# Two 512-column weight pieces in place of four, and the second block's transposes ahead of the first gate quarters

## The chip, the cores and the metric

The kernel runs on one core of one Trainium2 chip. The metric is the device time of one execution in microseconds. The kernel before took 236.01 us, the median of three runs that went from 235.99 to 237.07.

## What is computed

Three parts are added: the input x itself, a long convolution gated by the normalized input (part A), and a gated pair of projections (part B). S is 2048 rows, D is 640, F is 1728, all in bf16.

```python
def _A_ref(q, k, v, shift_k, ssm_k, ssm_D):
    ...
    for t in range(ks):
        k_shift = k_shift + k_pad[:, t:t + S, :] * shift_k[:, ks - 1 - t][None, None, :]
    kv = k_shift * v
    ...                    # y: kv convolved with ssm_k along S, by FFT over 2S
    y = y + kv * ssm_D[None, None, :]
    return q * y

def _B_ref(x, w_gate, w_up, w_down):
    g = jnp.einsum("bsd,df->bsf", x, w_gate)
    u = jnp.einsum("bsd,df->bsf", x, w_up)
    h = _sigmoid(g) * u
    return jnp.einsum("bsf,fd->bsd", h, w_down)

x = A_q
xn = _layernorm(x, axis=-1)
return x + _A_ref(xn, A_k, A_v, A_shift_k, A_ssm_k, A_ssm_D) + _B_ref(xn, B_w_gate, B_w_up, B_w_down)
```

## The kernel before

**Part B.** The 2048 rows are 16 blocks of 128. Four blocks make a group (t = 0 to 3). For a group, xn is transposed into xnT (for each block five pieces of 128 channels), and for each of 13 slices of 128 weight columns (fc) there is a gate product and an up product, each five matmuls of 128x512 (product, L260), into tiles pg and pu of the PSUM ring psG, which has four buffers. ScalarE takes the sigmoid of pg (gate_ev, L269), VectorE multiplies it by pu into hT (up_ev, L275). A last slice holds the remaining 64 columns of both matrices (both_mm, L281). Then hT goes through w_down (down_mm, L304), and VectorE adds the result to x (L309). Weights stay in SBUF: w holds gate and up columns, wd the rows of w_down.

**Part A.** The columns are five chunks of 128 (c). VectorE makes kv from k, the taps sc and v (kv_op, L337 to L346) and turns the filter hn (h_turn, L323). The convolution is done by transforms on TensorE in two steps each way (st1_mm L363 and L365, st2_mm L396, inv1_mm L425, inv2_mm L464), evicted by ScalarE (L223) or VectorE (L226), with trips through DRAM between them on SP's queue (wr1 L377, rd2 L387, wr2 L441, rdb L455).

**The start.** SP and ScalarE load the four blocks of group 0 (L479, L481). SP then loads the weight columns 0 to 255 and 256 to 511 of gate and of up (load_w, L173 and L176). TensorE has nothing to do yet: busy(10), L491, issues ten matmuls on a zeroed tile whose result is not used. VectorE normalizes the four blocks one after the other: statistics (L198), their mean (L202), the variance (L210), the power -1/2 on GpSimd (L214), and xn (ln_xn, L219). turn(i) is five transposes of block i on TensorE (xn_mm, L233) and a copy of their PSUM tile into xnT by ScalarE (xn_ev, L236). For group 0 the first two weight slices are not done as five matmuls of 512 columns but in quarters of 128 columns, one block at a time (quarter, L251), so that they can begin before all four blocks are there: quarters(0, i) is ten gate matmuls of block i, quarters(1, i) ten up matmuls. On TensorE the order is: turn(0), five more matmuls of busy, quarters(0,0), turn(1), quarters(0,1), turn(2), quarters(1,0), quarters(1,1), turn(3), quarters(0,2), quarters(1,2), quarters(0,3), quarters(1,3). Then the products of slice 2 begin. ScalarE's copy for block 1 is what quarters(0,1) waits for.

**The order of the rest.** Every later step belongs to a chain that is named by a letter: g are TensorE's products, s and u their evictions, m the first loads on SP's queue, l the normalization and so on. A string, ORDER, written out by hand, says whose next step is issued; each engine executes its steps in that order. The chain m holds the loads of the weight columns from 512 on (in pieces of 256, gate and up in turn), the taps sraw of chunk 0 (load_taps, L143), the small table SMt, w_down, k (L155, L159, L160), the filter, v, the table S1t and the next group's x (L129). SP's queue also carries the transposes of xn for the later groups (xn_turn, L240).

Of the kernel before, what the change touches and what calls it, by code (L numbers as in the profile page):

```python
# [57 lines left out]
def kernel(  # L58
# [62 lines left out]
    sync = nc.sync  # L121
# [108 lines left out]
    def xn_mm(i):  # L230
        xts[i] = pt = psC.tile([P, NC, P], BF16, name="pt", tag="c")
        for c in range(NC):
            nc.tensor.transpose(pt[:, c, :], xn[:, i, c * P:(c + 1) * P], ident[:])  # L233

    def xn_ev(i):
        nc.scalar.copy(out=xnT[:, i, :, :], in_=xts[i][:, :, :])  # L236
# [8 lines left out]
    def quarter(u, fc, i):  # L245

        if i == 0:
            pgs[u, fc] = psG.tile([P, 512], F32, name=("pg", "pu")[u], tag="g")
        o = u * UP + fc * P
        for c in range(NC):  # L250
            nc.tensor.matmul(pgs[u, fc][:, i * P:(i + 1) * P], lhsT=w[:, c, o:o + P], rhs=xnT[:, i, c, :],  # L251
                             start=(c == 0), stop=(c == NC - 1))
# [236 lines left out]
    def busy(n):  # L489
        for _ in range(n):  # L490
            nc.tensor.matmul(idle[:, :], lhsT=hT[:, 0, 0:P], rhs=hT[:, 0, :], start=True, stop=True)  # L491

    def turn(i):
        xn_mm(i)
        xn_ev(i)
# [9 lines left out]
        ln_pow(0, i, i + 1)  # L505
    ln_xn(0, 3)
    turn(0)
    busy(5)
    def quarters(u, i):
        quarter(u, 0, i)  # L510
        quarter(u, 1, i)

    for i in range(2):
        quarters(0, i)
        turn(i + 1)
    for i in range(2):
        quarters(1, i)
    turn(3)
    for i in range(2, 4):
        for u in range(2):  # L520
            quarters(u, i)
# [7 lines left out]
    def step(k, fn, *args):  # L529
        chains[k].append((fn, args))  # L530
# [16 lines left out]
    def hs(c):  # L547
        return [(load_h, c)]

    def ks(c):  # L550
        return [(load_halo, c), (load_k, c, 0, 8), (load_k, c, 8, NB)]

    def vs(c):
        return [(load_v, c, 0, 8), (load_v, c, 8, NB)]

    for k in ((load_w, sync, 512, 768, 0),
              (load_w, sync, 512, 768, 1),
              (load_taps, 0),
              (sync.dma_start, SMt[:], SMd.ap()),
              (load_w, sync, 768, 1024, 0),  # L560
              (load_w, sync, 768, 1024, 1),
              (load_w, sync, 1024, 1280, 0),
              (load_w, sync, 1024, 1280, 1),
              (load_wd, sync, 0, 7),
              *ks(0),
              (load_w, sync, 1280, FF, 0),
              (load_w, sync, 1280, FF, 1),
              *hs(0),
              *vs(0),
              (load_wd, sync, 7, NFC),  # L570
              (sync.dma_start, S1t[:], S1d.ap()),
              *hs(1),
              (load_x, sync, 1),
              *ks(1),
              *vs(1)):
        step("m", *k)
# [59 lines left out]
    step("o", store, NB - 1, NB, 4 * P, DM)  # L636

    ORDER = """
    mmggmmsmgmmuggmsgmgsuZumgggssumkgkguskugkkmsgugmmmmgkgmksgmuggHskkHkgsmukkgDumsgggkusumgmkgkukagaumH
    gTlllAKlglAatkwuAmmmakPlAkgalAklkwgalggagkegeugADkkaeAaAgewaugkuAHkuggkAukTkwsgKkgkkgnustakguKKgghal  # L640
    AsukwAsakggrluglsaksAugHggkAVubkkkBlswKBukgggaTVsgpkuslukawgDkHPlngAaAaskgAKrwAkukgspbgtkkBsllBugauA
    kgagpsAaguswVpakAguhkHHAgrgDkwcgVklguCkkraeCagAgkAbuBkuBkkggKgkbBKpggBaeualwukkggeIuurlTlAegkwtVbBBg
    gagkAagppswuAaghkuaKswgpAAkaHAskWgHupDgakuVsAggswucglJukkgkrClrsbngpBugaBaAgAWkkgsbspugPkrBgwpgsRFku
    kgprcwgCJusgbgusgpuBdBWppbqrgsdBlrRuqgBcqlCggJbsggksuBupgllkBbBgrqkWBgeaaeAAuppwdgaduRegaIAgrugpaAqa
    eqggupAwcCqpJguugdbgFBgbBqqgugBppdcpWCuJqgrpsgqbgBsuwFgrgqsbuBgpBRsuWgpdcpqqdguJgqCsrrbFBgsgRbugBBpd
    rsppugcdCqugCqgbsgWBqpqggusrBRbpudgrgqWspBpBqcupdJsgCbgRBpgBqqguWgsppuqscCudgJsguqgqgRdWgoquuqoddRgg
    gRqquqguoqoggdoouqdgdqgqdqqqugoggqqugoooouooo
    """
    left = {k: iter(v) for k, v in chains.items()}
    for k in "".join(ORDER.split()):  # L650
# [33 lines left out]
```

## Time and profile before

| what | value |
|---|---|
| median of three runs | 236.01 us |
| the profiled execution, its own time | 236.98 us |
| its span, from the first to the last instruction | 235.2 us |
| TensorE busy | 229.1 us (97%) |
| TensorE weight loads | 131.3 us (56%), beside the matmuls |
| VectorE busy | 204.5 us (87%) |
| ScalarE busy | 121.4 us (52%) |
| GpSimd busy | 12.4 us (5%) |
| moved by DMA | 56.79 MB, mean 241 GB/s |
| first product of 512 columns starts | 13.93 us |

Busy time is that of an engine's instructions; a TensorE matmul's end is modelled, since matmuls overlap in the pipe, so the spacing of their starts tells the pace better than their durations. PEclk in the page is the granted clock in tenths. The profile is of one execution; its time differs from the median of the runs by 0.97 us, so sums are made in the profiled execution and carried over as differences. In rows of the timeline the first number is the start in us from the start of the span, the second the duration, xN the number of instructions merged into the row, and the brackets hold the engine's idle time before the row and what ended it.

### The profile page before, as it was taken

Reading aid. Unit: us, or ns where it says so; the run is one execution under the profiler, and the core shown is the slowest. Engines: PE = TensorE matmul, PEld = TensorE weight load, DVE = VectorE, ACT = ScalarE, POOL = GpSimd, SP = SyncE. Lnnn points to the kernel's source line nnn. Section 1 sums busy time; section 2 is a strip of 40 time slices with the busy share of each in tenths; the row PEclk is TensorE's granted clock in tenths of the full one; section 3 lists DMA queues with packets and bytes.
Section 4 is the critical chain, followed back from the end, with each engine's and each line's share of the span. In section 5 each row is a group of like instructions: output and inputs, shape, how many; then the busy total and the mean of one; then the engine's idle time right before and its main releaser. Section 6 shows DMA issues by size and latency. Waiting matters only on the chain. (4 is left out here: it accounts for less than half of the span.)

```text
span 235.2 us, 5440 instructions
## 1 busy us (share of the span) xinstructions
PE 229.1 (97%) x2203; PEld 131.3 (56%) x2203; DVE 204.5 (87%) x364; ACT 121.4 (52%) x152; POOL 12.4 (5%) x24
## 2 busy tenths in 40 slices
PE   7899999999999999999999999999999999999995
PEld 2764445777454545677564544468754444446772
DVE  4633799999979999999999999997889999897773
ACT  2342332463555788575586747674446667762000
POOL 5210010020001010000000300000000000000000
PEclk9999999999999999999999999999999999999999
DMA  6999999698899999989899989986999777876884
GB/s 184 292 310 247 273 299 290 182 263 146 217 284 291 229 337 236 291 201 258 221 200 300 281 238 300 257 230 183 280 212 316 190 216 204 210 188 171 236 258 134
DMA packets 97615, 56.79 MB, mean 241 GB/s; under 512 B 55926, under 2 KB 91830, under 8 KB 97334
## 3 DMA queue, kind: packets, MB, share of 16 engines
q1 hardware_dynamic: 97158, 56.12, 90.9%
q10 hardware_dynamic: 432, 0.33, 0.7%
q8 instruction: 17, 0.28, 0.5%
q14 instruction: 8, 0.07, 0.1%
HBM read 36.12 MB, written 18.35 MB: 232 GB/s over the span
## 5 line engine op out<-in xcount | busy, mean ns | idle before, releaser
L260 PEld LDWEIGHTS <-w 128*128 128x128 bf16 x500 | 46.7, 98 | 54.4 <-issue 4.8
L304 PE MATMUL pd<-wd,hT 128*128 128x320 bf16 (+2 forms) x448 | 66.0, 299 | 0.0
L260 PE MATMUL pg<-xnT,w 128*128 128x512 bf16 x250 | 62.2, 379 | 0.2 <-ACT sig L269 0.2
L260 PE MATMUL pu<-xnT,w 128*128 128x512 bf16 x250 | 62.2, 379 | 0.0
L304 PEld LDWEIGHTS <-hT 128*128 128x128 bf16 x448 | 41.7, 98 | 18.2 <-issue 2.4
L223 ACT CAST t<-ps 128x1024 bf16<-128x1024 f32 x38 | 37.5, 1014 | 26.1 <-PE ps L365 15.2
L269 ACT ACTIVATE sig<-pg 128x512 bf16<-128x512 f32 x52 | 31.1, 602 | 28.7 <-PE pg L260 23.4
L275 DVE TENSOR_TENSOR hT<-sig,pu 128x512 bf16<-128x512 bf16 x52 | 35.0, 680 | 11.6 <-PE pu L260 7.5
L223 ACT CAST xz<-ps 128x1024 bf16<-128x1024 f32 x36 | 35.1, 1015 | 15.7 <-PE ps L396 15.6
L411 DVE TENSOR_TENSOR xz<-xz 128x2048 bf16<-128x2048 bf16 x20 | 24.4, 1220 | 0.2
L363 PE MATMUL ps<-kvh,S1t 128*128 128x128 bf16 x160 | 21.5, 218 | 0.6 <-ACT t L223 0.4
L365 PE MATMUL ps<-kvh,S1t 128*128 128x128 bf16 x160 | 21.6, 220 | 0.0
L343 DVE TENSOR_TENSOR acc<-acc,tmp 128x1024 bf16<-128x1024 bf16 x30 | 20.5, 684 | 0.3
L341 DVE TENSOR_TENSOR tmp<-kx,sc 128x1024 bf16<-128x1024 bf16 x30 | 20.4, 681 | 0.3
L309 DVE TENSOR_TENSOR x<-pd,x 128x320 bf16<-128x320 f32 (+2 forms) x32 | 15.2, 482 | 3.8 <-PE pd L304 3.6
L363 PEld LDWEIGHTS <-S1t 128*128 128x128 bf16 x160 | 15.5, 97 | 3.9 <-DVE kvh L346 1.6
L365 PEld LDWEIGHTS <-S1t 128*128 128x128 bf16 x160 | 15.4, 96 | 2.4
L198 DVE BATCH_NORM_STATS2 st<-x 128x6 f32<-128x320 bf16 x32 | 13.9, 475 | 2.5 <-DMA x<-in_A_q_dram 2.5
L469 DVE TENSOR_TENSOR yx<-psb,xn 128x512 bf16<-128x512 f32 x20 | 13.7, 686 | 1.4 <-PE psb L464 0.8
L409 DVE STREAM_SHUFFLE xz<-xz 128x512 f32<-128x512 f32 x20 | 14.5, 727 | 0.0
L223 ACT CAST ao<-psa 128x1024 bf16<-128x1024 f32 x9 | 9.0, 1013 | 8.4 <-PE psa L425 6.9
L464 PEld LDWEIGHTS <-TBt 128*128 128x128 bf16 x160 | 9.9, 98 | 3.4 <-issue 1.8
(48 smaller groups left out, 150.1 us busy)
## 6 DMA issues: line engine op xcount, KB each, us to landing
d<-t SPq DMA_DIRECT2D x20, 512.0 KB, 4.3
t<-d SPq DMA_DIRECT2D x20, 512.0 KB, 6.9
bi<-d SPq DMA_DIRECT2D x8, 512.0 KB, 4.7
d<-ao SPq DMA_DIRECT2D x6, 512.0 KB, 5.8
kx<-in_A_k_dram SPq DMA_DIRECT2D x10, 256.0 KB, 6.4
hn<-in_A_ssm_k_dram SPq DMA_DIRECT2D x20, 128.0 KB, 4.8
kvh<-in_A_v_dram SPq DMA_DIRECT2D x10, 256.0 KB, 5.4
x<-in_A_q_dram SPq DMA_DIRECT2D x3, 640.0 KB, 7.4
```

Of the source, the lines that this page charges most:

```text
L223: nc.scalar.copy(out=out, in_=in_)
L260: nc.tensor.matmul(pg[:, :], lhsT=w[:, c, u * UP + fc * P:u * UP + (fc + 1) * P], rhs=xnT[:, :, c, :], start=(c == 0), stop=(c == NC - 1))
L269: nc.scalar.activation(sig[fc][:, :], pgs[0, fc][:, :], ACT.Sigmoid)
L275: nc.vector.tensor_tensor(hT[:, fc, :], sig[fc][:, :], pgs[1, fc][:, :], ALU.mult)
L304: nc.tensor.matmul(pd[:, :], lhsT=hT[:, fc, bb * P:(bb + 1) * P], rhs=wd[:, fc, es], start=(fc == 0), stop=(fc == NFC - 1))
L309: nc.vector.tensor_tensor(x[:, 4 * t + bb, es], pds[bb, half][:, :], x[:, 4 * t + bb, es], ALU.add)
L341: nc.vector.tensor_tensor(d["tmp"][:, :, :], kx[:, lo + 3 - m:hi + 3 - m, :], sb(m), ALU.mult)
L343: nc.vector.tensor_tensor(d["acc"][:, :, :], d["acc"][:, :, :], d["tmp"][:, :, :], ALU.add)
L363: nc.tensor.matmul(ps[:, i, 0:P], lhsT=S1[:, b, h, :], rhs=cin[c]["kvh"][:, 0, b, :], start=True, stop=True)
L365: nc.tensor.matmul(ps[:, i, P:2 * P], lhsT=S1[:, b, h, :], rhs=hp[:, b // 2, b % 2, :], start=True, stop=True)
L409: nc.vector.stream_shuffle(z[:, 2, :, :].bitcast(F32), z[:, 1, :, :].bitcast(F32), swap)
L411: nc.vector.tensor_tensor(z[:, 1:3, :, :], z[:, 0:1, :, :].to_broadcast((P, 2, 8, P)), z[:, 1:3, :, :], ALU.mult)
```

## The change

Three edits, and no step is put elsewhere in ORDER except that two m steps are gone with the loads that they stood for.

- busy(5) becomes busy(3).
- turn(1) goes ahead of quarters(0,0) and quarters(0,1). The order on TensorE is now: turn(0), three matmuls of busy, turn(1), quarters(0,0), quarters(0,1), turn(2), quarters(1,0), quarters(1,1), turn(3), and from there as before.
- The weight columns 512 to 1023 are loaded in one piece for each matrix, both ahead of sraw and SMt. Before, columns 512 to 767 of both stood ahead of sraw and SMt, and columns 768 to 1023 of both behind them.

```diff
     turn(0)
-    busy(5)
+    busy(3)
...
-    for i in range(2):
-        quarters(0, i)
-        turn(i + 1)
-    for i in range(2):
-        quarters(1, i)
-    turn(3)
+    turn(1)
+    for u in range(2):
+        for i in range(2):
+            quarters(u, i)
+        turn(2 + u)
     for i in range(2, 4):
         for u in range(2):
             quarters(u, i)
...
-    for k in ((load_w, sync, 512, 768, 0),
-              (load_w, sync, 512, 768, 1),
+    for k in ((load_w, sync, 512, 1024, 0),
+              (load_w, sync, 512, 1024, 1),
               (load_taps, 0),
               (sync.dma_start, SMt[:], SMd.ap()),
-              (load_w, sync, 768, 1024, 0),
-              (load_w, sync, 768, 1024, 1),
               (load_w, sync, 1024, 1280, 0),
               (load_w, sync, 1024, 1280, 1),
...
-    mmggmmsmgmmuggmsgmgsuZumgggssumkgkguskugkkmsgugmmmmgkgmksgmuggHskkHkgsmukkgDumsgggkusumgmkgkukagaumH
+    mmggmmsmgmuggmsgmgsuZumgggssumkgkguskugkkmsgugmmmmgkgmksgmuggHskkHkgsmukkgDumsgggkusumgmkgkukagaumHgT
...
```

## The prediction

> **What bounds the kernel now.** I read the page's busy shares and clock first, then the chain that ended last, the waits, the timeline of the first 14 us, and last the long stretches without idle time.
>
> ```profile
> PE 229.1 (97%) x2203; PEld 131.3 (56%) x2203; DVE 204.5 (87%) x364; ACT 121.4 (52%) x152; POOL 12.4 (5%) x24
> PEclk9999999999999999999999999999999999999999
> PE 49%; DVE 0%; issue 0%
> ```
>
> TensorE is busy 97% of the span at the full granted clock, and the chain that ended last is matmuls almost alone. So time is saved where TensorE idles, runs slowly, or does work that the result does not need. The waits of PE name three of 0.4 us or more: the start itself, one in the front that the change rewrites, and one at 56 us:
>
> ```profile
> PE idle L491 <- DVE hT L117: 1.2, 1, 1.2
> PE pg L251 <- ACT xnT L236: 0.8, 1, 0.8
> PE ps L363 <- ACT t L223: 0.4, 1, 0.4
> ```
>
> The timeline shows the front (start, duration, engine, line, operation, count; idle time in brackets):
>
> ```profile
> 6.40 1.44 PE L491 MATMUL idle<-hT 128*128 128x512 bf16 x5
> 6.90 0.43 DVE L219 TENSOR_SCALAR xn<-x,mv,rstd 128x640 bf16<-128x640 bf16 x1
> 7.68 0.72 PE L251 MATMUL pg<-xnT,w 128*128 128x128 bf16 x10
> 8.24 0.44 PE L233 MATMUL pt<-ident,xn 128*128 128x128 bf16 x5
> 8.72 0.69 ACT L236 COPY xnT<-pt 128x640 bf16<-128x640 bf16 x1 [1.38 <-PE pt L233]
> 9.46 0.72 PE L251 MATMUL pg<-xnT,w 128*128 128x128 bf16 x10 [0.78 <-ACT xnT L236]
> 11.69 0.72 PE L251 MATMUL pg<-xnT,w 128*128 128x128 bf16 x10
> 13.93 1.24 PE L260 MATMUL pg<-xnT,w 128*128 128x512 bf16 x5
> ```
>
> The normalized block 1 is ready at 6.90 + 0.43 = 7.33, but its transposes stand behind five warming matmuls (idle, L491) and ten quarter matmuls, and start at 8.24. ScalarE's copy of them ends at 9.41, and PE idles for it. From 13.93 the products follow each other at 1.08 us for five matmuls with no gap until 55.6.
>
> What becomes of a gain at 13.93 is decided further on, where VectorE has almost no idle time:
>
> ```profile
> 31.46 0.69 DVE L275 TENSOR_TENSOR hT<-sig,pu 128x512 bf16<-128x512 bf16 x1
> 50.93 6.38 SPq L240 DMA_TRANSPOSE xnT<-xn  x4
> 59.35 0.46 SPq L155 DMA_DIRECT2D kx<-in_A_k_dram  x1
> 61.77 3.08 SPq L159 DMA_DIRECT2D kx<-in_A_k_dram  x1
> 66.04 0.69 DVE L337 TENSOR_TENSOR acc<-kx,sc 128x1024 bf16<-128x1024 bf16 x1 [1.48 <-DMA kx<-in_A_k_dram]
> 67.66 0.89 DVE L198 BATCH_NORM_STATS2 st<-x 128x6 f32<-128x320 bf16 x2 [0.33 <-DMA x<-in_A_q_dram]
> ```
>
> By the table of stretches DVE is busy 32.46 of the 33.0 us from 31.5 to 64.5, and 47.00 of 47.80 us from 67.7 to 115.5. At 31.46 it is released by PE. Its xn at 50.32 to 50.87 releases SP's transposes at 50.93; behind those SP issues, back to back, the kx and x loads of 59.35 and 59.86, which land 7 to 8 us later and release DVE at 66.04 and 67.66. PE waits for DVE's kvh again by 116. So end and front are tied by a chain PE, DVE, SP, DMA, DVE, PE, each link started by the one before.
>
> **The change, part by part.**
>
> 1. *Two warming matmuls fewer, block 1's turn ahead of the quarters.* Narrow windows give the starts of the five warming matmuls: 6.40, 6.81, 7.03, 7.25, 7.46; the clock rises at the second. With three, PE is free at 7.25. The first turn's transposes began 0.05 after their xn; so block 1's go at 7.33 + 0.05, say 7.42 with their weight load. Five transposes issue in 5 x 0.056 = 0.28, until 7.70. ACT starts its copy 0.48 after the first transpose (8.24 to 8.72) and takes 0.69: 7.90 to 8.59.
> 2. *The quarters, in order.* Ten issue in 0.56 (11.69 to 12.25). quarters(0,0) runs 7.70 to 8.26 (xnT of block 0 is there at 6.64 + 0.69 = 7.33). Then PE waits for 8.64: 0.38 us of stall is left of some 0.94 between issues. quarters(0,1) to 9.20, turn(2) to 9.48 (its xn was ready at 8.78), the twenty up quarters to 10.60, turn(3) to 10.88 (xn ready at 10.20), forty quarters in 2.24 (as from 11.69 to 13.93): **13.12**. The copies for turn(2) and turn(3) would end at 10.37 and 11.77, and are needed at 10.88 and 12.00. The front is 13.93 - 13.12 = **0.81 us** shorter: 0.26 from the warming (0.43 for two, less 0.17 waiting for xn) and 0.55 from the stall.
> 3. *Bounds of it.* In this execution the clock rose at 6.8. Were it up before 5.89, the old front would be quicker: transposes to 6.17, five warming matmuls to 7.25, quarters to 7.81, turn(1)'s copy ended 8.98, so 0.43 earlier, while the new one stays held by xn at 7.33: gain 0.4. With a somewhat later rise both stretch, the old one by two more slow matmuls (2 x 0.21): gain up to 1.2.
> 4. *Weight pieces.* Four loads of 320 KB with 512 B rows become two of 640 KB with 1 KB rows. SP loses two issues (0.43 and 0.56), which no one waits for. The old pieces passed at 293 GB/s (10 to 11 us); wd, with 1280 B rows, at 359 and 364 (17 to 19 us). 1.31 MB take 4.47 us at the one pace and 3.60 at the other: everything behind comes 0 to 0.87 earlier; I take 0.7, near the longer rows. The wait for a whole piece costs nothing: at worst pace the gate piece lands when two old ones had (6.55 + 6.0 = 12.6), the up piece by 15.4 (9.89 + 5.5), and column 512 is first used at 18.25 - 0.81 = 17.4. Without that cover it would stall PE by the difference, 4.8 us away.
> 5. *What moves back.* sraw and SMt go behind 640 KB more, by at most 2.2 us; GpSimd's copy of sraw (13.07 to 13.71) is needed by DVE at 23.44, and nothing stands behind it before 31 us.
> 6. *What must come earlier too.* The first kx half lands at 16.67 + 6.2 = 22.9. DVE took it at 23.44 and would want it at 22.6. With 0.7 from point 4 it is there; with nothing, DVE waits 0.25, and its idle 0.27 + 0.87 + 0.14 + 0.14 before 31.46 takes that in. The x load of 37.41 lands by about 43.2, wanted at 44.53 - 0.81 = 43.7. In 44 to 46 us the DMA share is 0.16: the load stream of the front has ended there and cannot hold what follows. No stall of point 1 to 5 is late next; the chain told above moves as a whole.
>
> **Sum:** -0.81. The profiled execution took 236.98 (span 235.2, and 1.8 around it), so it would be 236.17. It was slower by 0.97 than the median of 236.01; taken from the median, **235.2**.
>
> **The rivals.**
>
> *A. The gain is eaten on the way* (236.0). A late load, or DVE's full stretch from 31.5, holds the old times. For it: DVE has 0.54 us of slack in 33. Against: it starts on PE's release, and its loads have 0.5 us or more. 0.15.
>
> *B. More than the front* (234.2). PE's later gaps between issues, read from the matmul starts in narrow windows, 0.59 at 55.6, 0.40 at 63.2, 0.32 at 87, 0.22 at 90 and 0.31 at 115.5, make 1.8 us; they hang on DVE and on loads. If the shorter loads take half of DVE's 1.8 us of idle time at 64.6 to 67.7 away and about 1.0 of these gaps go, it is 0.81 + 1.0. For it: DVE is full behind that idle time. Against: it is released by SP's order, not by load volume. 0.13.
>
> *C. The clock comes later* (236.3). Slow matmuls issue at 0.107 for 128 columns and 0.427 for 512, fast ones at 0.056 and 0.216. With two warming matmuls fewer and transposes in their place, the rise could miss 6.8. If it came only as turn(2) starts, the front would run: three warming matmuls to 7.68, turn(1) to 8.21, quarters to 9.28 and 10.35, turn(2) 10.63, then 11.75, 12.03 and 14.27: 0.34 behind the old 13.93. It loses from a rise at 9.6 on. The rows speak against: the rise at 6.8 comes before anything the change moves. 0.07. *The Trainium skill, "TensorE: Matmul & The Clock Gate", Part 1, says the clock is decided in free-running windows of about 3.4 us, and Part 4 says that transposes don't count as busy in them; by that rule the next chance after 6.8 would be 10.2, which comes to nearly the same price. The trace agrees that five transposes ran at 0.107 at 5.89, but shows the rise after them all the same.*
>
> *D. Slower: the kx and x loads of 59.35 miss their turn* (237.8). SP issues in order, and a full queue makes one issue long: the halo load at 61.77 took 3.08 us against 0.46 for the kx load. If, with the phases shifted, such a block of 2.6 us comes ahead of the kx load, DVE restarts 2.6 later at 66, cannot catch up (0.8 us idle in 48), and PE waits by 116: -0.81 + 2.6 = +1.8. It decides from 0.8 us on, and is slower by 0.5% from 2.0 on. For it: this part is crowded. Against: all that fills the queue there hangs on the same chain and moves along. 0.10.
>
> *E.* That the change does nothing can't be: the five transposes do move ahead of the ten quarters on PE. The late piece (point 4) is 4.8 us away and counted in D's share.
>
> **How the numbers follow.** Forecast 0.55, A 0.15, B 0.13, C 0.07, D 0.10. 0.5% is 1.18 us, about what a measurement can tell from no change. Faster by more: B and the edge of the forecast, 0.15. Slower by more: D, 0.10. The rest within: 0.75. The range runs from B's 234.2 over A and C to 236.5, leaving out D and a little of B.
>
> **What would show it.** In the profile after: transposes of block 1 at about 7.4, the stall before quarters(0,1) near 0.4, the first 512-column product at about 13.1, the kx load landing by 22.9, DVE's waits for kx and x near 65.2 and 66.9, and the same later stalls, 0.8 earlier. I am wrong in the front if the copy or the clock makes the product start after 13.5, and wrong behind it if the lead at 31 us is not there at 68 or at 116.

## The result, and the profile after

The changed kernel took 236.18 us (median of 22 runs, 235.01 to 237.31), the kernel before 236.71 us on the same occasions (22 runs, 235.62 to 238.15). The ratio is 0.9973 with a 95% interval of 0.996 to 0.9986: 0.64 us faster (0.33 to 0.95). That is a gain, and smaller than the 0.81 us of the forecast, though 0.81 lies in the interval. The three runs from which the forecast counted down had a median of 236.01; over 22 runs it was 0.7 us higher, and the absolute figure of 235.2 came out 1.0 us too low.

The page after, busy times, granted clock and the chain that ended last:

```profile
PE 228.3 (97%) x2200; PEld 131.2 (56%) x2201; DVE 204.8 (87%) x364; ACT 121.6 (52%) x152; POOL 12.4 (5%) x24
PEclk9999999999999999999999999999999999999999
PE 79%; DMA 11%; DVE 3%; SPq 3%; ACT 2%; issue 1%; ACTq 0%
```

TensorE's work is less by two warming matmuls and else the same (the third matmul fewer is one of L304 that this trace lacks). The chain, followed back further than in the page before, goes through DMA for 11% of the span: loads and stores release what releases TensorE.

The front of the profile after, in rows of the timeline:

```profile
6.18 0.87 PE L491 MATMUL idle<-hT 128*128 128x512 bf16 x3
6.89 0.43 DVE L219 TENSOR_SCALAR xn<-x,mv,rstd 128x640 bf16<-128x640 bf16 x1
7.38 0.45 PE L233 MATMUL pt<-ident,xn 128*128 128x128 bf16 x5 [0.33 <-DVE xn L219]
7.67 0.72 PE L251 MATMUL pg<-xnT,w 128*128 128x128 bf16 x10
7.87 0.69 ACT L236 COPY xnT<-pt 128x640 bf16<-128x640 bf16 x1 [0.75 <-PE pt L233]
8.61 0.72 PE L251 MATMUL pg<-xnT,w 128*128 128x128 bf16 x10 [0.22 <-ACT xnT L236]
10.84 0.72 PE L251 MATMUL pg<-xnT,w 128*128 128x128 bf16 x10
13.08 1.24 PE L260 MATMUL pg<-xnT,w 128*128 128x512 bf16 x5
```

Block 1's transposes start 0.06 us after its xn, the copy is out at 8.56, and the first product starts at 13.08 (forecast 13.12, before 13.93). VectorE's row of 31.46 stands at 30.62, so the lead of 0.84 us is there. In this one execution it did not reach the end: the span is 235.1 after 235.2. The waits of PE, and VectorE's restart, tell where it went:

```profile
PE ps L363 <- ACT t L223: 1.3, 1, 1.3
PE ps L396 <- DMA t<-d: 0.9, 2, 0.6
...
PE pg L251 <- ACT xnT L236: 0.2, 1, 0.2
```

```profile
30.62 0.69 DVE L275 TENSOR_TENSOR hT<-sig,pu 128x512 bf16<-128x512 bf16 x1
...
64.58 0.69 DVE L337 TENSOR_TENSOR acc<-kx,sc 128x1024 bf16<-128x1024 bf16 x1 [0.68 <-DMA kx<-in_A_k_dram]
...
66.30 0.49 DVE L198 BATCH_NORM_STATS2 st<-x 128x6 f32<-128x320 bf16 x1 [0.42 <-DMA x<-in_A_q_dram]
```

The stage-1 matmuls at 56.3 waited 1.3 us for ScalarE, against 0.4 before, so the lead was gone there. VectorE restarted at 64.58 and 66.30, 1.46 and 1.36 earlier than before, so it was back at 66; the wait for t<-d at 129.86 took 0.60 of it again. Such single waits differ between executions of one kernel: in a second profile of the changed kernel (e5) the wait at 55.6 is 0.55 us, and the span is 233.9. One profile shows where time can go, and the medians say what a change is worth.

### The profile page after: what moved, and what is told of

Read it like the earlier page. It is cut to its first block, busy times and chain, and to the rows that moved or that the text cites. A ratio compares the mean times of both kernels' runs of the same rounds, so it can differ in the third digit from the quotient of the medians.

```text
span 235.1 us, 5433 instructions
## 1 busy us (share of the span) xinstructions
PE 228.3 (97%) x2200; PEld 131.2 (56%) x2201; DVE 204.8 (87%) x364; ACT 121.6 (52%) x152; POOL 12.4 (5%) x24
## 2 busy tenths in 40 slices
DMA packets 96303, 56.79 MB, mean 242 GB/s; under 512 B 55894, under 2 KB 90518, under 8 KB 96022
## 4 chain that ended last, share of the span: by engine, by line
PE 79%; DMA 11%; DVE 3%; SPq 3%; ACT 2%; issue 1%; ACTq 0%
PE pd L304 23%; PE pg L260 19%; PE pu L260 19%; PE psb L464 4%; DMA d<-ao 4%; PE ps L363 3%; PE ps L365 3%; DMA d<-t 3%; DMA t<-d 3%; PE ps L396 3%; PE psa L425 2%; DMA x<-in_A_q_dram 2%; PE pg L281 2%; ACT t L223 1%; SPq L169 1%; PE pu L251 1%
## 5 line engine op out<-in xcount | busy, mean ns | idle before, releaser
L304 PE MATMUL pd<-wd,hT 128*128 128x320 bf16 (+2 forms) x447 | 65.9, 299 | 0.1
L304 PEld LDWEIGHTS <-hT 128*128 128x128 bf16 x448 | 41.7, 98 | 18.2 <-issue 2.4
```

Source lines behind the costliest of these rows:

```text
L304: nc.tensor.matmul(pd[:, :], lhsT=hT[:, fc, bb * P:(bb + 1) * P], rhs=wd[:, fc, es], start=(fc == 0), stop=(fc == NFC - 1))
```

## The experiments

Medians in us; each ratio is to the kernel before on the same chip and occasion, with its 95% interval.

| run | median | before | ratio (interval) |
|---|---|---|---|
| e1 front only | 236.73 | 236.50 | 1.0018 (0.9989 to 1.0047) |
| e2 pieces only | 236.42 | 236.50 | 0.9999 (0.9974 to 1.0025) |
| e3 changed, five warming matmuls | 236.05 | 236.50 | 0.9989 (0.9966 to 1.0012) |
| e4 before, thirteen warming matmuls | 238.69 | 236.50 | 1.0089 (1.0067 to 1.0111) |
| e5 changed, again | 235.85 | 236.61 | 0.9970 (0.9956 to 0.9984) |
| e6 front only, again | 236.78 | 236.61 | 1.0003 (0.9984 to 1.0023) |
| e7 changed, wider t tiles | 235.97 | 236.61 | 0.9977 (0.9960 to 0.9993) |
| e8 before, wider t tiles | 236.49 | 236.61 | 0.9991 (0.9976 to 1.0006) |
| e9 changed, one load more | 236.72 | 236.63 | 1.0012 (0.9985 to 1.0039) |
| e10 before, one load more | 237.84 | 236.63 | 1.0071 (1.0047 to 1.0096) |
| e11 changed, no warming after turn(0) | 236.02 | 236.63 | 0.9966 (0.9947 to 0.9986) |
| e12 front only, half table | 235.87 | 236.46 | 0.9982 (0.9959 to 1.0006) |
| e13 before, half table | 236.07 | 236.46 | 0.9988 (0.9971 to 1.0005) |
| e14 changed, half table | 235.50 | 236.46 | 0.9965 (0.9940 to 0.9989) |

### The parts alone, and a dose of delay (e1 to e4)

e1 takes the first two hunks of the change (busy(3) and the order of turn and quarters) and leaves the loads; e2 takes the loads and leaves the front; e3 and e4 change one number:

```diff
# e3, in the changed kernel          # e4, in the kernel before
-    busy(3)                         -    busy(5)
+    busy(5)                         +    busy(13)
```

> Only the new order of the front (three warming matmuls, block 1's turn ahead of the first quarters); the weight loads stay in pieces of 256 columns. Theory 1 (the front gain passes whole to the end, the pieces give nothing by themselves): first 512-column product at 13.1, end 0.8 us earlier than before, ratio 0.9965. Theory 2 (the gain is eaten in part at 55 us, where stage 1 waits for the store d<-t to land): product at 13.1, the stall at 55 us over 1.2 us, end 0.2 to 0.5 earlier, ratio 0.998 to 0.999. Theory 3 (the gain at the end comes from the larger pieces): product at 13.1, end as before, ratio 1.000.

> Only the weight columns 512 to 1023 in one piece per matrix; the front's order and five warming matmuls as before. Theories 1 and 2: the kx load lands 0.6 us earlier, first product still at 13.9, end within 0.2 us of before, ratio 0.999 to 1.001. Theory 3: end 0.4 to 0.7 us earlier, ratio 0.997 to 0.998.

> The changed kernel with five warming matmuls in place of three. Working of the prediction: PE is free at 7.68 in place of 7.42, so the first product is 0.26 later than in the changed kernel, at 13.35, and by theory 1 the end is 0.55 us earlier than before, ratio 0.9977; by theory 2 under 0.4 earlier, ratio over 0.998.

> The kernel before with eight warming matmuls more (13 in place of 5) after the first turn: a dose of delay at the front, 8 x 0.216 = 1.73 us, first product at 15.66. Theory 1 (what is gained or lost at the front passes whole to the end): 1.7 us slower, ratio 1.0073. Theory 2 (later waits take up part of a shift): under 1.1 us slower, ratio under 1.0045, with shorter stalls at 55 us and 63 us.

The front alone gained nothing, although its first product started at 13.01. Theory 1 said 0.9965, which is outside the interval. The pieces alone showed no gain either, but their interval reaches from 0.6 us faster to 0.6 us slower, so e2 by itself does not exclude theory 3, that the pieces give the gain. Neither edit by itself shows the gain of the two.

In e4 the delay was smaller than worked out: the first product came at 14.97, not at 15.66. That is 7.77 us after block 1's xn, 1.2 to 1.5 more than in the profiles with five warming matmuls (6.24 to 6.60). The end came 2.1 us later (1.6 to 2.6), so the delay passed whole, and probably more than whole: the profile has waits of TensorE of 0.7 us for kvh and 1.4 for t<-d that the one before lacks. What delays the front reaches the end; what shortens it reaches it only if something else comes along.

e3 cannot be told from the changed kernel, nor, by its interval, from the kernel before. Its first product came at 13.04, not at 13.35. The clock rose at 6.14 in this execution, in the profile before at 6.79, so the five warming matmuls were through by 7.25, before block 1's transposes started at 7.33. The 0.26 us of point 2, worked out for the later rise, are not tested by it.

### Is it the wait at 55 us? (e5 to e8)

e5 and e6 repeat the changed kernel and the front alone on one chip. e7 and e8 give ScalarE's copies more room:

```diff
         if n % 2 == 0:
-            d[n // 2] = cv.tile([P, 8, 2, P], BF16, name="t1", bufs=2)
+            if c < 2 and n >= 4:
+                d[n // 2] = TB[:, n // 2 - 2, :, :].rearrange("p (b s) c -> p b s c", s=2)
+            else:
+                d[n // 2] = cv.tile([P, 8, 2, P], BF16, name="t1", bufs=2)
```

> The changed kernel once more, beside the front's order alone on one chip. Theory 1 (front gain passes whole): 0.5 to 0.8 us faster than before, ratio 0.9965 to 0.998, and no more executions over 237.1 us than the kernel before has (3 of 29 so far). Theory 2 (eaten at the wait for the store d<-t at 55 us): ratio over 0.998, the stall at 55 us over 1 us in the profile.

> The front's order alone, again. Its first set had two groups, 235.6 to 236.3 us and 237.1 to 238.6 us, six each. Theory 1 alone cannot say that; it expects ratio 0.9965 and no second group. Theory 4 (with small pieces and an earlier TensorE, a late load costs 1 to 2 us in about half of the executions, and larger pieces prevent it): two groups again, median ratio 0.999 to 1.003. If the first set was chance: one group near 236.0.

> The changed kernel, in which the third and fourth stage-1 tile of chunks 0 and 1 lie in the not yet loaded table TBt, so that ScalarE's copies at 55 us need not wait for the store d<-t of the first tile to land. Theory 2: the stall of 1.5 us at 55 us goes, and the end is 0.8 us or more earlier than before, ratio under 0.9965. Theory 1: the stall goes, but DVE and the loads behind it set the end, ratio as of the changed kernel, 0.997 to 0.998.

> The kernel before with the same wider tiles. Theory 2: its stall at 55 us (0.6 us) goes; it gains up to 0.5 us, and the difference to the changed kernel with wider tiles is the whole 0.8 us of the front. Theory 1: no gain (ratio 0.999 to 1.001), and the difference to the changed kernel with wider tiles is 0.5 to 0.8 as without them.

The changed kernel repeated its gain, and the front alone its lack of one; their medians, taken on one occasion, are 0.9 us apart. The two groups of executions that e6 was to show again did not come: its twelve runs spread from 235.69 to 237.97. Theory 2 fell: e7 came to 0.9977, where it expected less than 0.9965. With wider tiles ScalarE no longer waits for the store, but PE then waits for VectorE's kvh at the same place, and nothing is gained. The wait row of e7:

```profile
PE ps L363 <- DVE kvh L346: 1.0, 2, 0.6
```

What the front alone lacks stands in the profile of e6. Rows of VectorE's timeline, the first load of kx, then hn and x of the next chunk and group:

```profile
23.20 0.69 DVE L337 TENSOR_TENSOR acc<-kx,sc 128x1024 bf16<-128x1024 bf16 x1 [0.83 <-DMA kx<-in_A_k_dram]
...
43.57 1.11 DVE L323 STREAM_TRANSPOSE kvh<-hn 128x512 f32<-128x512 f32 x1 [1.13 <-DMA hn<-in_A_ssm_k_dram]
45.15 0.89 DVE L198 BATCH_NORM_STATS2 st<-x 128x6 f32<-128x320 bf16 x2 [0.48 <-DMA x<-in_A_q_dram]
```

VectorE waits for three loads. In the profile before and in the one after it waits for none of the three. The same rows of the profile before:

```profile
23.44 0.69 DVE L337 TENSOR_TENSOR acc<-kx,sc 128x1024 bf16<-128x1024 bf16 x1
...
43.50 1.10 DVE L323 STREAM_TRANSPOSE kvh<-hn 128x512 f32<-128x512 f32 x1
44.53 0.84 DVE L198 BATCH_NORM_STATS2 st<-x 128x6 f32<-128x320 bf16 x2
```

With the front 0.8 us earlier and the loads where they were, VectorE has become the one that waits. The reader should note the size: VectorE is free for hn at 42.44, 1.06 earlier than before, but starts on it 0.07 later than before (43.57 against 43.50), and on x 0.62 later (45.15 against 44.53). The DMA rows of the issues from 34 us on say why (KB each, median us from issue to landing). First the kernel before, then e6:

```profile
hn<-in_A_ssm_k_dram SPq DMA_DIRECT2D x4, 128.0 KB, 4.3
```

```profile
hn<-in_A_ssm_k_dram SPq DMA_DIRECT2D x4, 128.0 KB, 7.5
```

SP issues hn when VectorE lets it, so earlier here (the first at 34.47, before at 35.62); but the 1 MB of S1t stands in the queue ahead, and the four loads took 7.5 us in place of 4.3. The last landed at 43.54, before at 41.38. The stream arrives later than in the kernel before, not only too late for the new front; why it does, with the same loads in the same order, these rows do not show.

How the lateness reaches TensorE is seen in e6 too. ScalarE's copy of the next chunk's taps (L151) waits for its load, in the profile before it does not, and TensorE then waits for ScalarE and for VectorE:

```profile
46.74 0.65 ACT L151 COPY sc<-sraw 128x512 bf16<-128x512 bf16 x1 [2.26 <-DMA sraw<-in_A_shift_k_dram]
```

```profile
PE ps L363 <- ACT t L223: 1.2, 1, 1.2
PE ps L363 <- DVE kvh L346: 0.8, 1, 0.8
```

These two waits, at 48.35 and 56.79, are 2.0 us, against 0.5 in e5. The first product of e6 started 0.34 us earlier than that of e5, and its span is 1.0 us longer (234.9 against 233.9): 1.5 less 0.34 is 1.2, so the waits account for the difference. A wait of 0.7 to 0.9 us for kvh stands in the profiles of e1, e6, e9 and e10, in which VectorE waits for hn, and in e4; without the wider tiles of e7 and e8, no other profile has it. This is what theory 4 says.

### Lengthening and shortening the load stream (e9 to e14)

e9 and e10 add a load that nobody reads; e11 takes the warming away; e12 to e14 load half of the table S1t and use it twice:

```diff
# e9, e10: behind the first two loads of the chain m
+              (sync.dma_start, TB[:, 0, 0:10, :].rearrange("p (c b) x -> p c (b x)", c=5), wgr[:, :, 512:768]),
# e11
-    busy(3)
# e12, e13, e14
-              (sync.dma_start, S1t[:], S1d.ap()),
+              (sync.dma_start, S1t[:, 0:8], S1d.ap()[:, 0:8]),
...
-            nc.tensor.matmul(ps[:, i, 0:P], lhsT=S1[:, b, h, :], ...
+            nc.tensor.matmul(ps[:, i, 0:P], lhsT=S1[:, b % 8, h, :], ...
```

> The changed kernel with one more load behind the two large pieces: 320 KB of w_gate in 512 B rows into the table TBt, which is free until later; nobody reads it. It puts back into the load stream somewhat more time (1.1 us) than the larger pieces took out of it (0.75). Theory 4 (the front's gain reaches the end only if the load stream of the first 45 us comes earlier as well; otherwise VectorE waits for the first kx at 22.6, for hn and x at 42 to 44): these three waits appear, together over 0.8 us, and the gain is gone, ratio 0.9995 to 1.004. Theory 1 (the loads have slack): ratio 0.997 to 0.998 as the changed kernel.

> The kernel before with the same load of 320 KB more. By the profile before, VectorE wants kx at 23.44 (landed 22.9), hn at 43.5 (landed 41.4) and x at 44.5 (landed 43.2), so 1.1 us can be taken up but for 0.6 us at kx, which the idle time up to 31 takes in. Theory 4: under 0.4 us slower, ratio 0.9995 to 1.002, less than the same load costs in the changed kernel (0.5 us or more). If the load costs as much here, it is the load itself and not its meeting the earlier front.

> The changed kernel without any warming matmul after the first turn. With the new order the first product has started 5.76 us after xn of block 1 was ready in every profile, with three or five warming matmuls and the clock's rise anywhere between 3.8 and 6.3 us: the warming is off the path. Theory 1: ratio as the changed kernel, 0.997 to 0.998. Rival C (the clock misses its rise when TensorE has less to do): in some executions rise after 7.5 us, first product after 13.5, ratio 0.998 to 1.000.

> The front's new order with the small pieces, and only the first half of the table S1t loaded (512 KB in place of 1 MB) and used twice, so stage 1 computes with the wrong half for blocks 8 to 15; all instructions stay. The half table takes about 1.3 us out of the load stream just ahead of hn and x, and nothing ahead of the first kx. Theory 4 (the small pieces cost the front its gain because hn and x arrive late at 42 to 44 us): these waits go, the wait for kx stays at 0.3 to 0.8 and is taken in by 31 us, and the gain appears, ratio 0.9965 to 0.998. If the small pieces hurt in another way: ratio 0.999 to 1.003 as before.

> The kernel before with the half table. In its profile VectorE does not wait between 31.5 and 64.5 us. Theory 4: nothing to win in most executions, ratio 0.998 to 1.000, and 0.4 us or more behind the front's new order with the half table. If it gains 0.6 us or more, the load stream bounds the kernel before as well in its usual execution.

> The changed kernel with the half table. Theory 4: the larger pieces have already taken the waits away, so the half table gives it 0.3 us at most, ratio 0.996 to 0.9975, equal to the front's new order with the half table. A ratio under 0.995 would say that the load stream still costs the changed kernel time before 45 us.

e9 took the gain away, as theory 4 said, and the three waits came back (0.95 at kx, 1.64 at hn, 0.40 at x in its rows). e10 is the miss: under 0.4 us was expected, less than in the changed kernel, and the kernel before lost 1.7 us (1.1 to 2.3), where the changed kernel lost about 1.0 (1.0012 after 0.9970). Its profile shows the same waits:

```profile
24.05 0.69 DVE L337 TENSOR_TENSOR acc<-kx,sc 128x1024 bf16<-128x1024 bf16 x1 [1.07 <-DMA kx<-in_A_k_dram]
...
44.41 1.10 DVE L323 STREAM_TRANSPOSE kvh<-hn 128x512 f32<-128x512 f32 x1 [0.76 <-DMA hn<-in_A_ssm_k_dram]
46.00 0.49 DVE L198 BATCH_NORM_STATS2 st<-x 128x6 f32<-128x320 bf16 x1 [0.48 <-DMA x<-in_A_q_dram]
```

By the profile before, hn has 2.1 us of slack (landed 41.4, wanted 43.5); a load of 1.1 us should not use it up. It did: hn now takes 6.5 us from issue to landing in place of 4.3. Here the slack of a load that stands behind others in a full queue was not its landing subtracted from its use. Some of the difference can lie between executions: in e8, with the loads of the kernel before, the last hn landed at 42.08. TensorE waits 1.4 us for ScalarE and 0.7 for kvh in e10, much as in e6. So the price is paid in both kernels, and the control was none: by the condition set for e10, e9 shows the cost of the load itself, not of its meeting the earlier front. The kernel before is itself close to the edge of its load stream.

The half table is the complement. In e12 hn lands 3.8 us after its issue, and VectorE starts it without a wait, while the wait for kx stays:

```profile
22.87 0.69 DVE L337 TENSOR_TENSOR acc<-kx,sc 128x1024 bf16<-128x1024 bf16 x1 [0.45 <-DMA kx<-in_A_k_dram]
...
42.40 1.10 DVE L323 STREAM_TRANSPOSE kvh<-hn 128x512 f32<-128x512 f32 x1
43.43 0.84 DVE L198 BATCH_NORM_STATS2 st<-x 128x6 f32<-128x320 bf16 x2
```

ScalarE's wait for the taps and TensorE's for kvh are gone as well; what is left at this place is 0.5 us for ScalarE, as in e5. Against the kernel before of its own occasion, the front alone goes from 0.2 us slower (e1, e6) to 0.6 faster with the half table. The rows so show that the late loads at 42 to 46 us hold TensorE up, and that they go with the load ahead of them. The medians are less sharp: the kernel before gains 0.4 us from the half table too (e13), and e12 is only 0.2 us ahead of it, where 0.4 or more was expected. With the large pieces and the half table (e14) the median is 0.6 us ahead of e13, about the front's gain, and 0.4 ahead of e12, to which it was to be equal. The intervals of all three overlap.

## Why the prediction was right or wrong

**The front (points 1 and 2): right in its sum.** The first product came at 13.08 for 13.12, the stall before quarters(0,1) shrank to 0.38 between issues, as worked out. How the 0.81 divides hangs on the clock. With five warming matmuls (e3) the first product came 5.76 us after block 1's xn was ready, with three (after) or with none (e11) the same: in these executions the warming was through in time, the block's xn set the start, and the order of turn(1) is the whole gain. In the profile of e14 the third warming matmul still came 0.43 us behind the second (6.57 and 7.00), at the slow pace; block 1's transposes started at 7.24, 0.22 after its xn, and the distance is 5.92. So fewer warming matmuls count when the clock rises late, as it did in the execution of the forecast.

**The bounds of the front (point 3): right, and the step to the sum ignored them.** In five profiles with the old front and five warming matmuls the same distance is 6.24 (e8, e10) to 6.60 us (e13, before; e2 has 6.55), and the clock's rise, by the trace's record of the granted clock, goes with it: at 3.97 and 6.03 us in the first pair, from 6.35 to 6.79 in the others (the page's PEclk row does not show it: it has a 9 from the start, although matmuls of 512 columns issue every 0.427 us until the rise). So, with 5.76 for the new front, its gain is 0.48 to 0.84 from one execution to the next, and the one from which the sum was made, with its rise at 6.79, lay at the upper end. **This is the mis-sized term: 0.81 for a mean of some 0.68.** The measured 0.64 agrees with that.

**The step from the profile to the median failed, and it is the larger part of the error.** The prediction took the profiled execution, 236.98, for slow by 0.97 and counted 0.81 down from the median of three runs, 236.01. The 22 runs put that base at 236.71, so the profiled execution was slow by 0.27 only. Of the 0.98 us between 235.2 and the measured 236.18, 0.70 come from the base. The other 0.28 are the 0.81 of the forecast less the 0.53 between the two medians.

**The weight pieces (points 4 and 6): the pace was right, the conclusion wrong.** The stream ran at 321 GB/s from 6 to 12 us (291 before), the kx load came 0.6 earlier (16.08 + 6.2 = 22.3), and the pieces were in time. But the prediction gave the pieces no share of the gain, because every load that it looked at seemed to have slack enough without them: VectorE would wait 0.25 for kx, "and its idle 0.27 + 0.87 + 0.14 + 0.14 before 31.46 takes that in", and "The x load of 37.41 lands by about 43.2, wanted at 44.53 - 0.81 = 43.7." e1 and e6 are that case. VectorE waited 0.4 and 0.5 us for x and 0.2 and 1.1 for hn, and ScalarE 1.1 and 2.3 for sraw. The failed step is point 6: it took the landing of x over unchanged from the profile before and left out hn and sraw. hn, issued 0.9 and 1.2 us earlier than before, landed at 42.79 and 43.54, later than before (41.38).

**Rival A** (the gain eaten by a late load) is what the front's edit does without the pieces. In the changed kernel it is held off. **Rival B:** VectorE's idle time at 64 to 67 us shrank from 1.81 to 1.10 in the profile after and 1.04 in e5, and the end gained nothing beyond the front. **Rival C:** the rise at 6.83 in e11, without any warming after the first turn, cost nothing. Transposes issue every 0.056 us after the rise (7.38 to 7.67 for five) and at 0.107 before it. The Trainium skill, "TensorE: Matmul & The Clock Gate", Part 1, says that the rise depends on where a free-running window meets the first matmul, within half a microsecond about 4 us; in the 14 profiles that record it, it came 2.7 to 5.7 us after the first matmul at 1.18, so the traces agree that it varies and show a wider spread. **Rival D** did not come: kx and x landed earlier, relative to their chain too.

**The chain behind the front** passed a shift whole when it was a delay (e4). The prediction's picture, in which a shift moves everything along, holds in that direction only: a lead must be matched by the loads, which run by their own time.

What stays open: how much of the gain the pieces would give by themselves (e2 leaves up to 0.6 us), and why the loads land later when only the front is changed. No version was found that is clearly faster than the changed kernel: e11 is the same within its interval.

## What to carry to other kernels

When a front is shortened, list the loads that run by their own time, those that ScalarE waits for too, and move them by as much; two edits that gain nothing alone can gain together. Read the slack of a load from a run in which it is late: here a load behind a full queue landed 2.9 us later for 1.1 us put ahead of it. Make a sum for several executions when a term hangs on something that differs between them (here the clock's rise), and count down from a median of many runs.

## What the runs showed of the hardware that was not expected

Rows of 512 B moved at 291 GB/s and the mix with 1 KB rows at 321 in the same 6 us of the start, both with the DMA engines busy throughout. The Trainium skill, "DMA: Bandwidth & Descriptors", Specifications, gives 512 B as the least size for line rate; the runs differ, and go on gaining above it.

A load of 320 KB more at 7 us (1.1 us of the stream) made the hn loads at 36 us land about 2.9 us later (41.4 to 44.3 for the last), in one profile of each kernel. In the profiles in which hn was late (e1, e6, e9, e10), the fetch of instructions (16 KB on a queue of its own, 0.9 to 1.1 us for its one packet) came at 36.0 to 36.3, while S1t was still moving, and some packets of S1t were then seen long after the rest: in e6 most were through by 37.9 and the last by 40.1. In the profile before, the fetch came at 37.26, and the last packet of S1t was through by 37.55. The profile after has the same in a weaker form (the fetch at 36.23, most packets through by 36.9, the last by 38.5), and hn came in time. Whether the fetch causes the delay was not tried and stays open.
